# Centring a weight matrix on TensorE: full rows by zero padding, the gain in the conversion, another order of the first loads

## The chip, the cores and the metric

The kernel runs on one core of a Trainium2 chip. The metric is the device time of one launch in microseconds, the median of several runs. Below, PE is TensorE, ACT is ScalarE, DVE is VectorE, POOL is GpSimd and SP is SyncE; PEld is the weight load of a matmul.

## The reference, cut to what matters

The input x has 8 batches of 4224 rows of 192 numbers. First comes a causal convolution over rows: 7 taps, one set for each of 8 heads of 24 columns, made from `weight` by a softmax. Then a block with a layer norm, two matmuls and a residual:

```python
w = softmax(weight)                       # 8 heads x 7 taps
x = conv(x_padded_with_6_zero_rows, w)    # 8 x 4224 x 192
mu = mean(x); var = mean((x - mu)**2)
xn = (x - mu) / sqrt(var + 1e-6) * g_ln
out = x + max(xn @ w_ch1, 0) @ w_ch2      # 192 -> 768 -> 192
```

`w_ch1` and `w_ch2` come as 64-bit floats and are brought to 32 bits on the chip.

## The kernel before, in words

**Tiling.** A batch is laid out with 33 successive rows of x to each of the 128 partitions. Work goes in groups of up to 11 of these rows per partition; the first batch is cut into groups of 7, 8, 9 and 9, every other into three of 11, which makes 25 groups. For a group g the steps are: load x with 6 rows of halo (`load_x`, L91 to L107), convolve on DVE (`conv`, L245, y), transpose in blocks of 32 on DVE (`transpose`, L266, yt), multiply by w1 on PE (`up`, L315, matmul L325, four matmuls on 32 rows each beside one another, PSUM tiles ph), ReLU out of PSUM on ACT (L330, ht), multiply by w2 on PE (`down`, L335, matmul L348, PSUM tiles po), and add `rstd` times that to y on DVE (L353). `stats` (L274) computes rstd on DVE. The ReLU commutes with the positive factor rstd, so the norm's division comes last.

**Set-up.** The mean's subtraction and the gain g are folded into w1: w1 = (I - 1/192) diag(g) w_ch1, computed once by PE in `centre_w1` (L222). w_ch1 has 192 rows: the upper 128 lie in slots 1 and 2 of w1f (left and right half of the columns), the lower 64 in slot 0, the left half of the columns in partitions 0 to 63, the right half in 64 to 127. The stationary operands are the matrices centre (L209 to L220): POOL writes -1/192 and the diagonal, and ACT multiplies them by g (L219). For each of 6 blocks f of 128 columns and each of 6 blocks c of outputs, one matmul takes 128 rows (L230) and one takes the 64 rows of slot 0 that belong to f (L233); ACT copies the sums out of PSUM (L237). The trace shows each 32-bit matmul of the program as two instructions on PE: 72 here are 144.

**Conversion.** `split_words` (L152) takes the high words apart, with three operations on DVE and two on ACT (high and scale); `join_words` (L171) puts them together in three operations on DVE, the last a multiplication (L180). It is done for slots 0 and 1 (names 1a), then slot 2 (1b), later for w2 (mant, power, high, scale without a number).

**Order.** Each engine works in the order of the program text. At the end of the function: `conv(0)`, `centre_w1()`, `transpose(0)`, the conversion of w2, then per group `load_x(g+2)`, (`conv(1)` ahead of `up(0)`), `up(g)`, `conv(g+1)`, `transpose(g+1)`, `stats(g)`, `down(g)`. For groups 0 and 1 the first tap of the convolution is on ACT (L254), otherwise on DVE (L256). PSUM tiles ps are 8 buffers in a ring, for pw, ph and po alike. Loads of w1 are issued by ACT, those of the taps, x and w2 by SP, those of g by POOL.

Of the kernel before, what the change touches and what calls it, by code (L numbers as in the profile page):

```python
# [7 lines left out]
F32 = mybir.dt.float32  # L8
# [3 lines left out]
ALU = mybir.AluOpType  # L12
# [4 lines left out]
def kernel(  # L17
# [35 lines left out]
    NF = F // P  # L53
    NC = D // C
    NQ = P // C
    FH = F // 2
# [4 lines left out]
    groups = []  # L61
# [14 lines left out]
    xr = x.rearrange("b (p r) d -> b p (r d)", p=P)  # L76
# [5 lines left out]
    ypool = ctx.enter_context(tc.tile_pool(name="y", bufs=3))  # L82
# [6 lines left out]
    xg = {}  # L89

    def load_x(g):  # L91
        b, j0, n = groups[g]
        t = xpool.tile([P, J + PAD, D], F32, tag="xg", name=f"xg{g}")
        xg[g] = t
        flat = t.rearrange("p j d -> p (j d)")
        if j0:
            nc.sync.dma_start(
                out=flat[:, 0 : (n + PAD) * D], in_=xr[b, :, (j0 - PAD) * D : (j0 + n) * D]
            )
            return  # L100
        nc.gpsimd.memset(t[0:1, 0:PAD, :], 0.0)  # L101
        nc.sync.dma_start(out=flat[:, PAD * D : (PAD + n) * D], in_=xr[b, :, 0 : n * D])
        for p0, p1 in ((16, P), (1, 16)):
            nc.sync.dma_start(
                out=flat[p0:p1, 0 : PAD * D],
                in_=xr[b, p0 - 1 : p1 - 1, (R - PAD) * D : R * D],
            )  # L107

    taps = consts.tile([P, H, K], F32, name="taps")
    ga = consts.tile([P, 1], F32, name="ga")
    gb = consts.tile([P, 1], F32, name="gb")
    raw1 = setup.tile([P, 3, FH, 2], U32, name="raw1")
# [5 lines left out]
    def load_w1(r):  # L121
        nc.scalar.dma_start(  # L122
            out=raw1[:, 1 + r, :, :].rearrange("p f w -> p (f w)"),
            in_=w1_words[0:P, 2 * FH * r : 2 * FH * (r + 1)],
        )

    nc.sync.dma_start(
        out=taps, in_=bass.AP(tensor=weight.tensor, offset=0, ap=[[0, P], [K, H], [1, K]])
    )
    load_w1(0)  # L130
    for r in range(2):
        nc.scalar.dma_start(  # L132
            out=raw1[Q * r : Q * r + Q, 0, :, :].rearrange("p f w -> p (f w)"),
            in_=w1_words[P:D, 2 * FH * r : 2 * FH * (r + 1)],
        )
    load_w1(1)
    load_x(0)
    nc.gpsimd.dma_start(out=ga, in_=g_col[0:P, :])
    for r in range(2):
        nc.gpsimd.dma_start(out=gb[Q * r : Q * r + Q, :], in_=g_col[P:D, :])  # L140
# [11 lines left out]
    def split_words(raw, name):  # L152
        n = raw.shape[1]
        hi = raw[:, :, 1]
        mant = setup.tile([P, n], I32, name="mant" + name)
        power = setup.tile([P, n], I32, name="power" + name)
        high = setup.tile([P, n], F32, name="high" + name)
        scale = setup.tile([P, n], I32, name="scale" + name)
        nc.vector.tensor_single_scalar(mant.bitcast(U32), hi, 0xFFFFF, op=ALU.bitwise_and)  # L159
        nc.scalar.activation(high, mant, AF.Relu, scale=2.0**-20, bias=1.0)  # L160
# [7 lines left out]
        nc.scalar.activation(scale, power, AF.Relu, scale=float(1 << 23), bias=low)  # L168
        return high, scale

    def join_words(dst, raw, high, scale):  # L171
        lo, hi = raw[:, :, 0], raw[:, :, 1]
        nc.vector.scalar_tensor_tensor(  # L173
            out=high, in0=lo, scalar=2.0**-52, in1=high, op0=ALU.mult, op1=ALU.add
        )
# [4 lines left out]
        nc.vector.tensor_tensor(dst, high, scale.bitcast(F32), op=ALU.mult)  # L180
# [12 lines left out]
    parts_a = split_words(raw1a, "1a")  # L193
# [3 lines left out]
    nc.vector.tensor_tensor(  # L197
        taps, taps, wsum.unsqueeze(2).to_broadcast([P, H, K]), op=ALU.mult
    )
    join_words(w1f[:, 0:2].rearrange("p s f -> p (s f)"), raw1a, *parts_a)  # L200
    parts_b = split_words(raw1b, "1b")
    join_words(w1f[:, 2], raw1b, *parts_b)

# [6 lines left out]
    for i, (gk, spans) in enumerate(((ga, ((0, P, 0),)), (gb, ((0, Q, P), (Q, P, P))))):  # L210
        m = setup.tile([P, NC, NQ, C], F32, name=f"centre{i}")
        nc.gpsimd.memset(m, -1.0 / D)
        for p0, p1, base in spans:
            nc.gpsimd.affine_select(
                out=m[p0:p1], in_=m[p0:p1], pattern=[[-C, NC], [0, NQ], [-1, C]],
                compare_op=ALU.not_equal, fill=1.0 - 1.0 / D, base=base, channel_multiplier=1,
            )
        flat = m.rearrange("p c q i -> p (c q i)")
        nc.scalar.mul(flat, flat, gk)  # L219
        centre.append(flat.rearrange("p (c o) -> p c o", c=NC))  # L220

    def centre_w1():  # L222
        for f in range(NF):
            r, o = divmod(f * P, FH)
            rows = slice(Q * r, Q * r + Q)
            for c0, c1 in ((0, 4), (4, NC)):
                pw = psum.tile([P, 512], F32, tag="ps", name=f"pw{f}_{c0}")
                for c in range(c0, c1):
                    dst = pw[:, (c - c0) * P : (c - c0 + 1) * P]
                    nc.tensor.matmul(  # L230
                        dst, centre[0][:, c, :], w1f[:, 1 + r, o : o + P], start=True, stop=False
                    )
                    nc.tensor.matmul(  # L233
                        dst, centre[1][rows, c, :], w1f[rows, 0, o : o + P],
                        start=False, stop=True,
                    )
                nc.scalar.copy(  # L237
                    w1[:, c0:c1, f * P : f * P + P],
                    pw[:, 0 : (c1 - c0) * P].rearrange("p (c f) -> p c f", f=P),
                )  # L240


    y, yt, rstd = {}, {}, {}

    def conv(g):  # L245
        n = groups[g][2]
        t = xg.pop(g)
        y[g] = ypool.tile([P, J, D], F32, tag="y", name=f"y{g}")
        for k in range(K):
            for h in range(H):  # L250
                cs = slice(h * GRP, h * GRP + GRP)
                tap = taps[:, h, k : k + 1]
                if k == 0 and g < 2:
                    nc.scalar.mul(y[g][:, 0:n, cs], t[:, 0:n, cs], tap)  # L254
                elif k == 0:
                    nc.vector.tensor_scalar(  # L256
                        out=y[g][:, 0:n, cs], in0=t[:, 0:n, cs], scalar1=tap, scalar2=None,
                        op0=ALU.mult,
                    )
                else:  # L260
                    nc.vector.scalar_tensor_tensor(  # L261
                        out=y[g][:, 0:n, cs], in0=t[:, k : k + n, cs], scalar=tap,
                        in1=y[g][:, 0:n, cs], op0=ALU.mult, op1=ALU.add,
                    )

    def transpose(g):  # L266
        n = groups[g][2]
        yt[g] = tpool.tile([P, J, NC, C], F32, tag="yt", name=f"yt{g}")
        nc.vector.transpose(  # L269
            yt[g][:, 0:n].rearrange("p j c t -> p (j c t)"),  # L270
            y[g][:, 0:n].rearrange("p j d -> p (j d)"),
        )
# [90 lines left out]
                done = end  # L363


    conv(0)
    centre_w1()
    transpose(0)
    parts = split_words(raw2, "2")
    join_words(w2flat, raw2, *parts)  # L370
    for g in range(NG):
        if g + 2 < NG:
            load_x(g + 2)
        if g == 0:
            conv(1)
        up(g)
        if g + 1 < NG:
            if g > 0:
                conv(g + 1)
            transpose(g + 1)  # L380
        stats(g)
        down(g)
# [30 lines left out]
```

## Time and profile before

| what | value |
|---|---|
| time, median of 3 runs | 1118.62 us (1118.46 to 1118.95) |
| the profiled execution, its own time | 1119.14 us |
| its span, first to last instruction | 1117.3 us |
| PE busy | 1092.0 us, 98% of the span |
| DVE busy | 822.5 us, 74% |
| ACT busy | 242.0 us, 22% |
| first matmul starts | 22.01 us into the span |

The profile is one execution. A row "22.01 0.80 PE pw L230 x2" of the chain of waits reads: from 22.01 us, for 0.80 us, PE wrote pw by line 230, two instructions. A row of the groups reads: line, engine, operation, output<-inputs, shapes, count, then busy us and mean ns of one, then the idle time of the engine just before them and who ended it. A row of the stretches reads: from:to, length, and per engine busy us and (x) the number of instructions, then the granted PE clock, the share of DMA engines at work and GB/s.

### The profile page before, as it was taken

The page shows a single profiled execution, that of the slowest core. Times are in us where ns is not written, and L with a number is a line of the kernel's source. Part 1 is how long each engine was busy: PE and PEld are TensorE (multiplying, and loading weights), DVE is VectorE, ACT ScalarE, POOL GpSimd, SP SyncE. Part 2 cuts the span into 40 slices and gives each one's busy share as a digit, 9 for nine tenths or more (in the row PEclk, how much of TensorE's full clock was granted, in tenths as well). Part 3 has the DMA queues.
Part 4 walks back from the last instruction along what each step waited for, and adds up shares of the span by engine and source line. Part 5 has one row for each costly group of instructions (what it writes and reads, how often), then busy time and mean ns, then how long its engine had stood idle before and what let it go on. Part 6 is the DMA issues. An engine that isn't in the chain of part 4 may idle for free.

```text
span 1117.3 us, 24334 instructions
## 1 busy us (share of the span) xinstructions
PE 1092.0 (98%) x10512; PEld 917.0 (82%) x10512; DVE 822.5 (74%) x2362; ACT 242.0 (22%) x638; POOL 14.7 (1%) x20
## 2 busy tenths in 40 slices
PE   2999999999999999999999999999999999999998
PEld 1679998897897887887987978978978879879878
DVE  4429888869669678688697696696696786886921
ACT  3132122213113113122122032131131230221220
POOL 2000000000000000000000000000000000000000
PEclk9999999999999999999999999999999999999999
DMA  6002012202202202202102012022022022020001
GB/s 233 1 1 79 28 63 93 93 6 96 100 1 100 100 1 101 100 1 100 68 33 101 33 68 100 1 100 100 1 101 100 1 100 98 4 101 39 1 40 39
DMA packets 10475, 70.56 MB, mean 63 GB/s; under 512 B 1416, under 2 KB 2440, under 8 KB 4736
## 3 DMA queue, kind: packets, MB, share of 16 engines
q1 hardware_dynamic: 9824, 67.83, 16.6%
q8 instruction: 82, 1.34, 0.5%
q10 hardware_dynamic: 448, 1.18, 0.4%
q14 instruction: 25, 0.20, 0.1%
q0 software_dynamic: 96, 0.00, 0.0%
HBM read 43.05 MB, written 25.95 MB: 62 GB/s over the span
## 4 chain that ended last, share of the span: by engine, by line
PE 98%; DMA 1%; DVE 1%; ACTq 0%; ACT 0%; issue 0%; DVEq 0%
PE po L348 47%; PE ph L325 46%; PE pw L230 2%; PE pw L233 2%; DMA raw<-in_moe_w_ch_dram 1%; DVE w1f L180 0%; ACT centre L219 0%; DVE scale1a L176 0%; DVE high1a L173 0%; DVE power1a L165 0%; DVE mant1a L159 0%; ACTq L132 0%; DVE power1a L161 0%; DVE y L353 0%; ACTq L122 0%
## 5 line engine op out<-in xcount | busy, mean ns | idle before, releaser
L348 PEld LDWEIGHTS po<-w,ht 128*128 128x128 f32 x3168 | 513.5, 190 | 13.3 <-issue 11.7
L348 PE MATMUL po<-w,ht 128*128 128x192 f32 x3168 | 522.5, 327 | 0.0
L325 PE MATMUL ph<-yt,w 32*128 32x352 f32 (+3 forms) x7200 | 520.8, 445 | 0.0
L325 PEld LDWEIGHTS ph<-yt,w 32*128 32x128 f32 x7200 | 367.6, 186 | 145.4 <-issue 5.6
L261 DVE SCALAR_TENSOR_TENSOR y<-xg,taps,y 128x264 f32<-128x264 f32 (+3 forms) x1200 | 473.8, 477 | 0.9 <-ACT y L254 0.9
L330 ACT ACTIVATE ht<-ph 128x352 f32<-128x352 f32 (+3 forms) x600 | 222.7, 457 | 791.6 <-PE ph L325 791.6
L353 DVE SCALAR_TENSOR_TENSOR y<-po,r,y 128x192 f32<-128x192 f32 x264 | 96.6, 413 | 230.0 <-PE po L348 226.9
L282 DVE BATCH_NORM_STATS2 st<-y 128x6 f32<-128x192 f32 x264 | 70.1, 340 | 0.0
L269 DVE STREAM_TRANSPOSE yt<-y 128x2112 f32<-128x2112 f32 (+3 forms) x25 | 57.3, 2290 | 0.9
L256 DVE TENSOR_SCALAR y<-xg,taps 128x264 f32<-128x264 f32 (+1 forms) x184 | 51.4, 351 | 0.0
L230 PE MATMUL pw<-w1f,centre 128*128 128x128 f32 x72 | 28.6, 501 | 22.0 <-ACT centre L219 22.0
L230 PEld LDWEIGHTS pw<-w1f,centre 128*128 128x128 f32 x72 | 18.0, 310 | 29.9 <-ACT centre L219 22.0
L233 PE MATMUL pw<-w1f,centre 64*128 64x128 f32 x72 | 28.5, 498 | 0.0
L173 DVE SCALAR_TENSOR_TENSOR high<-raw,high 128x1152 f32<-128x1152 uint32 x1 | 1.4, 1358 | 34.1 <-ACT high L160 34.1
L233 PEld LDWEIGHTS pw<-w1f,centre 64*128 64x128 f32 x72 | 18.0, 310 | 8.2 <-issue 7.9
L101 POOL MEMSET xg<- 1x1152 f32 x8 | 8.4, 1047 | 819.6 <-DVE y L261 819.3
L237 ACT COPY w<-pw 128x512 f32<-128x512 f32 (+1 forms) x12 | 5.8, 479 | 43.5 <-PE pw L233 43.5
L304 DVE TENSOR_TENSOR d<-r 128x11 f32<-128x11 f32 (+3 forms) x75 | 12.8, 170 | 2.6
L305 DVE SCALAR_TENSOR_TENSOR d<-d,v 128x11 f32<-128x11 f32 (+3 forms) x75 | 12.8, 170 | 2.6
L308 DVE SCALAR_TENSOR_TENSOR r<-d,r 128x11 f32<-128x11 f32 (+3 forms) x75 | 12.7, 170 | 2.6
L159 DVE TENSOR_SCALAR mant1a<-raw 128x768 uint32<-128x768 uint32 x1 | 0.6, 560 | 7.3 <-DMA raw<-in_moe_w_ch_dram 7.3
L254 ACT ACTIVATE y<-xg,taps 128x168 f32<-128x168 f32 (+1 forms) x16 | 5.6, 433 | 0.0
(48 smaller groups left out, 58.7 us busy)
## 6 DMA issues: line engine op xcount, KB each, us to landing
xg<-in_x_dram SPq DMA_DIRECT2D x14, 1632.0 KB, 9.3
out_dram<-y SPq DMA_DIRECT2D x20, 1056.0 KB, 4.9
xg<-in_x_dram SPq DMA_DIRECT2D x7, 1056.0 KB, 7.9
xg<-in_x_dram SPq DMA_DIRECT2D x8, 504.0 KB, 9.2
xg<-in_x_dram SPq DMA_DIRECT2D x2, 1440.0 KB, 11.2
out_dram<-y SPq DMA_DIRECT2D x2, 864.0 KB, 4.4
xg<-in_x_dram SPq DMA_DIRECT2D x1, 1344.0 KB, 12.7
raw<-in_moe_w_ch_dram SPq DMA_DIRECT2D x1, 1152.0 KB, 10.0
```

What stands on the lines that cost most here:

```text
L230: nc.tensor.matmul(dst, centre[0][:, c, :], w1f[:, 1 + r, o : o + P], start=True, stop=False)
L233: nc.tensor.matmul(dst, centre[1][rows, c, :], w1f[rows, 0, o : o + P], start=False, stop=True,)
L256: nc.vector.tensor_scalar(out=y[g][:, 0:n, cs], in0=t[:, 0:n, cs], scalar1=tap, scalar2=None, op0=ALU.mult,)
L261: nc.vector.scalar_tensor_tensor(out=y[g][:, 0:n, cs], in0=t[:, k : k + n, cs], scalar=tap, in1=y[g][:, 0:n, cs], op0=ALU.mult, op1=ALU.add,)
L269: nc.vector.transpose(yt[g][:, 0:n].rearrange("p j c t -> p (j c t)"), y[g][:, 0:n].rearrange("p j d -> p (j d)"),)
L282: nc.vector.bn_stats(out=st[:, j, :], in_=y[g][:, j, :])
L304: nc.vector.tensor_tensor(d, r, r, op=ALU.mult)
L305: nc.vector.scalar_tensor_tensor(out=d, in0=d, scalar=-0.5, in1=v, op0=ALU.mult, op1=ALU.mult)
L325: nc.tensor.matmul(ph[q][:, 0 : n * C], w1[rows, c, fs], t[rows, 0:n, c, :], start=(c == 0), stop=(c == NC - 1),)
L330: nc.scalar.activation(ht[g][:, f, 0:n, q, :], ph[q][:, 0 : n * C].rearrange("p (j t) -> p j t", t=C), AF.Relu,)
L348: nc.tensor.matmul(dst, t[:, f, j, :, :].rearrange("p q t -> p (q t)"), w2[:, f, :], start=(f == 0), stop=(f == NF - 1),)
L353: nc.vector.scalar_tensor_tensor(out=yg[:, j, :], in0=dst, scalar=rstd[g][:, j : j + 1], in1=yg[:, j, :], op0=ALU.mult, op1=ALU.add,)
```

## The change

The lower 64 rows no longer get matmuls of 64 rows. There are three centre matrices: the first for the upper 128 rows, the second for the lower rows with the left half (partitions 64 to 127 are zero), the third for the lower rows with the right half (partitions 0 to 63 are zero). Each matmul of `centre_w1` then reads 128 rows, and the zeros cancel what does not belong to f. The gain g no longer goes into the centre matrices on ACT, but into w1f on DVE: the last multiplication of `join_words` becomes `scalar_tensor_tensor` (high times g times scale), in two pieces of 384 columns for 1a, one for 1b. The loads of g are issued first on POOL. w1 comes by one transfer of the upper 128 rows and one of 64 rows from ACT, and one of 64 rows from SP, which stands ahead of x there. The halo of x at the start of a batch comes with the rows themselves, in one piece per partition (two transfers by partitions, and one for partition 0). The first tap is a function of its own; its call for group 1 stands ahead of the conversion of w2.

```diff
-        nc.sync.dma_start(out=flat[:, PAD * D : (PAD + n) * D], in_=xr[b, :, 0 : n * D])
         for p0, p1 in ((16, P), (1, 16)):
             nc.sync.dma_start(
-                out=flat[p0:p1, 0 : PAD * D],
-                in_=xr[b, p0 - 1 : p1 - 1, (R - PAD) * D : R * D],
+                out=flat[p0:p1, 0 : (PAD + n) * D],
+                in_=bass.AP(
+                    tensor=x.tensor, offset=(b * S + p0 * R - PAD) * D,
+                    ap=[[R * D, p1 - p0], [1, (PAD + n) * D]],
+                ),
             )
+        nc.sync.dma_start(out=flat[0:1, PAD * D : (PAD + n) * D], in_=xr[b, 0:1, 0 : n * D])
...
-    load_w1(0)
+    nc.scalar.dma_start(
+        out=raw1[:, 1:3].rearrange("p s f w -> p (s f w)"), in_=w1_words[0:P, :]
+    )
     for r in range(2):
-        nc.scalar.dma_start(
+        (nc.sync, nc.scalar)[r].dma_start(
             out=raw1[Q * r : Q * r + Q, 0, :, :].rearrange("p f w -> p (f w)"),
             in_=w1_words[P:D, 2 * FH * r : 2 * FH * (r + 1)],
         )
-    load_w1(1)
     load_x(0)
...
-        nc.vector.tensor_tensor(dst, high, scale.bitcast(F32), op=ALU.mult)
+        if gain is None:
+            nc.vector.tensor_tensor(dst, high, scale.bitcast(F32), op=ALU.mult)
+            return
+        n = dst.shape[1] // len(gain)
+        for i, g in enumerate(gain):
+            part = slice(n * i, n * i + n)
+            nc.vector.scalar_tensor_tensor(
+                out=dst[:, part], in0=high[:, part], scalar=g, in1=scale.bitcast(F32)[:, part],
+                op0=ALU.mult, op1=ALU.mult,
+            )
...
-    join_words(w1f[:, 0:2].rearrange("p s f -> p (s f)"), raw1a, *parts_a)
+    join_words(w1f[:, 0:2].rearrange("p s f -> p (s f)"), raw1a, *parts_a, (gb, ga))
     parts_b = split_words(raw1b, "1b")
-    join_words(w1f[:, 2], raw1b, *parts_b)
+    join_words(w1f[:, 2], raw1b, *parts_b, (ga,))
...
+    for i, (p0, p1, base) in enumerate(((0, P, 0), (0, Q, P), (Q, P, P))):
         m = setup.tile([P, NC, NQ, C], F32, name=f"centre{i}")
...
-        nc.scalar.mul(flat, flat, gk)
-        centre.append(flat.rearrange("p (c o) -> p c o", c=NC))
+        if p1 - p0 < P:
+            nc.gpsimd.memset(m[P - p1 : P - p0], 0.0)
+        nc.gpsimd.memset(m[p0:p1], -1.0 / D)
...
-                    nc.tensor.matmul(
-                        dst, centre[0][:, c, :], w1f[:, 1 + r, o : o + P], start=True, stop=False
-                    )
-                    nc.tensor.matmul(
-                        dst, centre[1][rows, c, :], w1f[rows, 0, o : o + P],
-                        start=False, stop=True,
-                    )
+                    for m, s, start in ((centre[0], 1 + r, True), (centre[1 + r], 0, False)):
+                        nc.tensor.matmul(
+                            dst, m[:, c, :], w1f[:, s, o : o + P], start=start, stop=not start
+                        )
...
+    first_tap(0)
     conv(0)
     centre_w1()
+    first_tap(1)
     transpose(0)
```

What moves on the engines is seen in their rows. ACT at the start of the program, before: after its loads of w1 (raw) it converts (1a, 1b), multiplies two centre matrices by g, takes the first tap of group 0 and begins to copy the centred w1 (w) out of PSUM.

```order
L122 DMA raw_84<-in_moe_w_ch_dram 128x768
L132 DMA raw_84<-in_moe_w_ch_dram 64x768 x2
L122 DMA raw_84<-in_moe_w_ch_dram 128x768
...
L168 ACTIVATE scale1b<-power1b,low 128x384
L219 ACTIVATE centre_140<-centre_140,ga 128x768
L219 ACTIVATE centre_146<-centre_146,gb 128x768
L254 ACTIVATE y_155<-xg_91,taps 128x7x24 x8
L237 COPY w_138<-pw_0_212 128x4x128
```

The same place with the change:

```order
L130 DMA raw_84<-in_moe_w_ch_dram 128x1536
L134 DMA raw_84<-in_moe_w_ch_dram 64x768
...
L166 ACTIVATE scale1b<-power1b,low 128x384
L255 ACTIVATE y_157<-xg_93,taps 128x7x24 x8
L240 COPY w_138<-pw_0_214 128x4x128
```

Four transfers have become two, and the two multiplications of centre are gone. ACT after the last copy of the centring, before: the two operations for w2 (high, scale), the first tap of group 1, the first ReLU.

```order
L237 COPY w_138<-pw_4_302 128x2x128
L160 ACTIVATE high_312<-mant_310 128x1152
L168 ACTIVATE scale_313<-power_311,low 128x1152
L254 ACTIVATE y_324<-xg_100,taps 128x8x24 x8
L330 ACTIVATE ht_381<-ph_0_0_382 128x7x32
```

And with the change:

```order
L240 COPY w_138<-pw_4_304 128x2x128
L255 ACTIVATE y_310<-xg_99,taps 128x8x24 x8
L158 ACTIVATE high_323<-mant_321 128x1152
L166 ACTIVATE scale_324<-power_322,low 128x1152
L334 ACTIVATE ht_383<-ph_0_0_384 128x7x32
```

The eight multiplications of the first tap of group 1 now stand ahead of the two for w2. On SP's queue the loads at the start, before: taps, x of group 0 in three transfers (xg_91), w2 (raw_85), x of group 1.

```order
L127 DMA taps<-in_weight_dram 128x56
L102 DMA xg_91<-in_x_dram 128x1344
L104 DMA xg_91<-in_x_dram 112x1152
L104 DMA xg_91<-in_x_dram 15x1152
L141 DMA raw_85<-in_moe_w_ch_dram 128x6x384
L97 DMA xg_100<-in_x_dram 128x2688
```

And with the change:

```order
L127 DMA taps<-in_weight_dram 128x56
L134 DMA raw_84<-in_moe_w_ch_dram 64x768
L103 DMA xg_93<-in_x_dram 112x2496
L103 DMA xg_93<-in_x_dram 15x2496
L110 DMA xg_93<-in_x_dram 1x1344
L139 DMA raw_85<-in_moe_w_ch_dram 128x6x384
L97 DMA xg_99<-in_x_dram 128x2688
```

A part of w1 (raw_84) stands ahead of x, and x of group 0 comes with its halo.

More of the change, by code (lines that the diff above doesn't have):

```diff
@@ L119 @@
     g_col = moe_g_ln.rearrange("(d o) -> d o", o=1)
-    def load_w1(r):
-        nc.scalar.dma_start(
-            out=raw1[:, 1 + r, :, :].rearrange("p f w -> p (f w)"),
-            in_=w1_words[0:P, 2 * FH * r : 2 * FH * (r + 1)],
-        )
+    nc.gpsimd.dma_start(out=ga, in_=g_col[0:P, :])
+    for r in range(2):
+        nc.gpsimd.dma_start(out=gb[Q * r : Q * r + Q, :], in_=g_col[P:D, :])
     nc.sync.dma_start(
@@ L129 @@
     )
-    load_w1(0)
+    nc.scalar.dma_start(
+        out=raw1[:, 1:3].rearrange("p s f w -> p (s f w)"), in_=w1_words[0:P, :]
+    )
     for r in range(2):
-        nc.scalar.dma_start(
+        (nc.sync, nc.scalar)[r].dma_start(
             out=raw1[Q * r : Q * r + Q, 0, :, :].rearrange("p f w -> p (f w)"),
@@ L135 @@
         )
-    load_w1(1)
     load_x(0)
-    nc.gpsimd.dma_start(out=ga, in_=g_col[0:P, :])
-    for r in range(2):
-        nc.gpsimd.dma_start(out=gb[Q * r : Q * r + Q, :], in_=g_col[P:D, :])
     nc.sync.dma_start(
@@ L169, in split_words, with join_words @@
         return high, scale
-    def join_words(dst, raw, high, scale):
+    def join_words(dst, raw, high, scale, gain=None):
         lo, hi = raw[:, :, 0], raw[:, :, 1]
@@ L209 @@
     centre = []
-    for i, (gk, spans) in enumerate(((ga, ((0, P, 0),)), (gb, ((0, Q, P), (Q, P, P))))):
+    for i, (p0, p1, base) in enumerate(((0, P, 0), (0, Q, P), (Q, P, P))):
         m = setup.tile([P, NC, NQ, C], F32, name=f"centre{i}")
[L212 to L216, printed above, removed]
-            )
-        flat = m.rearrange("p c q i -> p (c q i)")
-        nc.scalar.mul(flat, flat, gk)
-        centre.append(flat.rearrange("p (c o) -> p c o", c=NC))
+        if p1 - p0 < P:
+            nc.gpsimd.memset(m[P - p1 : P - p0], 0.0)
+        nc.gpsimd.memset(m[p0:p1], -1.0 / D)
+        nc.gpsimd.affine_select(
+            out=m[p0:p1], in_=m[p0:p1], pattern=[[-C, NC], [0, NQ], [-1, C]],
+            compare_op=ALU.not_equal, fill=1.0 - 1.0 / D, base=base, channel_multiplier=1,
+        )
+        centre.append(m.rearrange("p c q i -> p c (q i)"))
     def centre_w1():
@@ L224, in centre_w1 @@
             r, o = divmod(f * P, FH)
-            rows = slice(Q * r, Q * r + Q)
             for c0, c1 in ((0, 4), (4, NC)):
@@ L229, in centre_w1 @@
                     dst = pw[:, (c - c0) * P : (c - c0 + 1) * P]
-                    nc.tensor.matmul(
-                        dst, centre[0][:, c, :], w1f[:, 1 + r, o : o + P], start=True, stop=False
-                    )
-                    nc.tensor.matmul(
-                        dst, centre[1][rows, c, :], w1f[rows, 0, o : o + P],
-                        start=False, stop=True,
-                    )
+                    for m, s, start in ((centre[0], 1 + r, True), (centre[1 + r], 0, False)):
+                        nc.tensor.matmul(
+                            dst, m[:, c, :], w1f[:, s, o : o + P], start=start, stop=not start
+                        )
                 nc.scalar.copy(
@@ L243, with first_tap @@
     y, yt, rstd = {}, {}, {}
+    def first_tap(g):
+        n = groups[g][2]
+        y[g] = ypool.tile([P, J, D], F32, tag="y", name=f"y{g}")
+        for h in range(H):
+            cs = slice(h * GRP, h * GRP + GRP)
+            dst, src, tap = y[g][:, 0:n, cs], xg[g][:, 0:n, cs], taps[:, h, 0:1]
+            if g < 2:
+                nc.scalar.mul(dst, src, tap)
+            else:
+                nc.vector.tensor_scalar(out=dst, in0=src, scalar1=tap, scalar2=None, op0=ALU.mult)
     def conv(g):
@@ L247, in conv @@
         t = xg.pop(g)
-        y[g] = ypool.tile([P, J, D], F32, tag="y", name=f"y{g}")
-        for k in range(K):
+        for k in range(1, K):
             for h in range(H):
                 cs = slice(h * GRP, h * GRP + GRP)
[L252 to L264, printed above, removed]
+                nc.vector.scalar_tensor_tensor(
+                    out=y[g][:, 0:n, cs], in0=t[:, k : k + n, cs], scalar=taps[:, h, k : k + 1],
+                    in1=y[g][:, 0:n, cs], op0=ALU.mult, op1=ALU.add,
+                )
     def transpose(g):
@@ L378 @@
             if g > 0:
+                first_tap(g + 1)
                 conv(g + 1)
```

## Prediction

> **What bounds the kernel now.** The page comes first: PE is busy almost from its first instruction to the last, and the chain that ended last is PE.
>
> ```profile
> span 1117.3 us, 24334 instructions
> PE 98%; DMA 1%; DVE 1%; ACTq 0%; ACT 0%; issue 0%; DVEq 0%
> ```
>
> So a microsecond counts only if it is taken from PE's line: from the start until PE runs, from what PE does, or from a wait put into it. The chain of waits in order of time shows that line at the start, where the whole change lies.
>
> ```profile
> 1.76 12.48 DMA raw<-in_moe_w_ch_dram
> ...
> 18.59 0.96 DVE w1f L180
> ...
> 21.04 0.93 ACT centre L219
> ...
> 22.01 0.80 PE pw L230 x2
> ...
> 73.54 0.72 PE pw L233 x2
> 74.27 16.20 PE ph L325 x288
> 90.47 13.85 PE po L348 x84
> 104.32 15.75 PE ph L325 x288
> ```
>
> Until 14.24 us w1 arrives, until 19.55 DVE converts it, until 21.97 PE waits for ACT's centre. Centring takes 74.27 - 22.01 = 52.26 us for 144 instructions, 0.363 us each. Then come up(0), down(0) and, at 104.32, up(1). Is 0.363 us what such a matmul must take? The groups of the page answer it.
>
> ```profile
> L348 PEld LDWEIGHTS po<-w,ht 128*128 128x128 f32 x3168 | 513.5, 190 | 13.3 <-issue 11.7
> L348 PE MATMUL po<-w,ht 128*128 128x192 f32 x3168 | 522.5, 327 | 0.0
> L230 PE MATMUL pw<-w1f,centre 128*128 128x128 f32 x72 | 28.6, 501 | 22.0 <-ACT centre L219 22.0
> L233 PE MATMUL pw<-w1f,centre 64*128 64x128 f32 x72 | 28.5, 498 | 0.0
> ```
>
> L348 loads weights of the same 128x128 and streams 192 columns, in 522.5 / 3168 = 0.165 us each; pw streams 128 and takes 2.2 times as long. Two reasons can be read. First, PE's timeline by single instructions, and that of the weight loads:
>
> ```profile
> 26.46 0.58 PE L230 MATMUL pw<-w1f,centre 128*128 128x128 f32 x1
> 26.46 0.79 PE L230 MATMUL pw<-w1f,centre 128*128 128x128 f32 x2
> 25.73 0.50 PEld L233 LDWEIGHTS pw<-w1f,centre 64*128 64x128 f32 x2 [0.23 <-issue]
> ```
>
> Within a pair of one line the second matmul ends 27.25 - 27.04 = 0.21 us after the first. Between pairs, where 128 rows give way to 64 or back, weight loading stands idle for 0.23 us with nothing shown to wait for: there PE empties itself first. Second, up(0) by stretches of time, one line and one shape throughout:
>
> ```profile
> 74.20:76.60 2.40, 2.40 (x25) 2.27 (x29) 1.00 0.01 3
> 76.60:79.00 2.40, 2.40 (x32) 2.27 (x28) 1.00 0.00 0
> 79.00:81.40 2.40, 2.40 (x56) 2.40 (x52) 1.00 0.03 7
> ```
>
> At 79.0 us PE doubles its pace (32 to 56 in 2.4 us), though the clock column says 1.00 throughout; so up to there PE ran at half speed, through all of the centring. The Trainium skill, "TensorE: Matmul & The Clock Gate", Part 1, says that PE starts at half clock and is released after some 3.4 us of sustained work; here 52 us of broken work released nothing, and 4.8 us of dense work did.
>
> **The change part by part.**
>
> *The padded matmuls.* All 144 now use 128 rows, so the 0.23 us between pairs goes. At half speed one costs the 0.21 us inside a pair, at full speed 0.165 x 128 / 192 = 0.110 us, if the weight load hides as it does in L348. Upper bound for full speed: the whole 0.165, as L348 does the same load and more columns in that. I take 4.8 us at half speed (as up(0) needed), which is 4.8 / 0.21 = 23 instructions, and 121 x 0.110 = 13.3 us: 18.1 us against 52.26. Zeros cost nothing by the row count: 64 and 128 rows take 498 and 501 ns. And PE is already at speed in up(0): 57 instructions took 4.8 us there, later 2.4, so up(0) takes 16.2 - 2.4 = 13.8 us.
>
> *The start.* Two stretches of time (the last number is GB/s) and the issues of w1:
>
> ```profile
> 4.00:7.00 3.00, 0.00 (x0) 0.00 (x0) 0.50 (x2) 1.28 (x1) 2.85 (x4) 1.00 0.88 313
> 7.00:10.00 3.00, 0.00 (x0) 0.00 (x0) 0.12 (x1) 0.25 (x1) 1.07 (x2) 1.00 1.04 231
> raw<-in_moe_w_ch_dram ACTq DMA_DIRECT2D x2, 384.0 KB, 9.9
> raw<-in_moe_w_ch_dram ACTq DMA_DIRECT2D x2, 192.0 KB, 11.9
> ```
>
> DVE's timeline up to the first additions out of PSUM:
>
> ```profile
> 14.38 0.56 DVE L159 TENSOR_SCALAR mant1a<-raw 128x768 uint32<-128x768 uint32 x1 [7.25 <-DMA raw<-in_moe_w_ch_dram]
> 21.76 0.56 DVE L180 TENSOR_TENSOR w1f<-high1b,scale1b 128x384 f32<-128x384 f32 x1
> 23.22 14.76 DVE L261 SCALAR_TENSOR_TENSOR y<-xg,taps,y 128x168 f32<-128x168 f32 x48 [0.90 <-ACT y L254]
> 38.01 1.58 DVE L269 STREAM_TRANSPOSE yt<-y 128x1344 f32<-128x1344 f32 x1
> 39.52 0.72 DVE L159 TENSOR_SCALAR mant<-raw 128x1152 uint32<-128x1152 uint32 x1
> 75.77 1.36 DVE L173 SCALAR_TENSOR_TENSOR high<-raw,high 128x1152 f32<-128x1152 uint32 x1 [34.07 <-ACT high L160]
> 79.71 15.88 DVE L261 SCALAR_TENSOR_TENSOR y<-xg,taps,y 128x192 f32<-128x192 f32 x48
> 95.63 1.78 DVE L269 STREAM_TRANSPOSE yt<-y 128x1536 f32<-128x1536 f32 x1
> 97.33 1.88 DVE L282 BATCH_NORM_STATS2 st<-y 128x6 f32<-128x192 f32 x7
> 102.34 2.43 DVE L353 SCALAR_TENSOR_TENSOR y<-po,r,y 128x192 f32<-128x192 f32 x7
> ```
>
> w1 is 2 x 384 + 2 x 192 = 1152 KB, 1.18 MB; x of group 0 with halo is 13 x 192 x 4 bytes x 128, 1.28 MB. Had w1 the 313 GB/s from 4 us to itself, it would be there at 7.8; if all of x came with it at the mean of both stretches (272), at 13.0. I take the middle, 10.4, and mant1a at 10.6 instead of 14.38. Bounds: 8.4 (the loads of g, though first, need their time too) and 14.38 (no gain; all of w1 is now awaited at once, also what came later as 1b). Two pieces with gain in place of L180 (0.96): at most 2 x 0.56, +0.15 us. With ACT's multiplications gone, PE starts at w1f: 10.6 + (19.55 - 14.38) + 0.15 = 15.9 us, and centring ends at 34.1. POOL has the g loads ahead and three more operations (two memsets, one matrix); it was at work for only 1.07 us of 7 to 10, so some 3 us more end before 15.9.
>
> *What is late next.* DVE: conv(0) starts behind 1b, at 10.6 + (22.32 - 14.38) + 0.15 = 18.7, takes 14.8 and ends at 33.5; its transpose ends at 35.1. So up(0) starts at 35.1: the convolution, which had 35 us to spare, is last now, 1.0 us behind PE. Every microsecond of w1's landing counts one to one; PE's own cold time does not, up to 1.0 us.
>
> *The moved first tap of group 1.* Nothing that waits is in front of it but PE's last copy.
>
> ```profile
> 20.52 0.62 ACT L168 ACTIVATE scale1b<-power1b,low 128x384 int32<-128x384 int32 x1
> 74.30 0.37 ACT L237 COPY w<-pw 128x256 f32<-128x256 f32 x1 [2.31 <-PE pw L233]
> 74.57 1.17 ACT L160 ACTIVATE high<-mant 128x1152 f32<-128x1152 int32 x1
> 75.64 1.25 ACT L168 ACTIVATE scale<-power,low 128x1152 int32<-128x1152 int32 x1
> 76.78 2.86 ACT L254 ACTIVATE y<-xg,taps 128x192 f32<-128x192 f32 x8
> 79.55 1.06 ACT L330 ACTIVATE ht<-ph 128x224 f32<-128x224 f32 x4
> ```
>
> ACT ends copying at 34.5, the tap at 37.4, then high and scale (2.3) at 39.7; behind these queues the first ReLU, until 40.8. up(0) has written all 8 PSUM buffers after two of six blocks, at 35.1 + 2 x 2.3 = 39.7, and waits there for 1.1 us. It ends at 35.1 + 13.8 + 1.1 = 50.0. DVE takes w2 up 1.2 us after ACT began (as 74.57 to 75.77): 38.6, w2 done at 42.5 (3.94 later, as 75.77 to 79.71), in time for down(0) at 50.0, which ends at 63.85. Then conv(1) until 58.5, its transpose until 60.2 (in time for up(1)), stats until 65.2, and the additions out of PSUM until 67.5. up(1) starts at 63.85, and its second block, 15.75 / 6 = 2.6 us later at 66.5, needs the four buffers of po: a wait of 1.0 us. Before, those were free at 104.77, for 106.95. So up(1) is as if started at 64.85, against 104.32: 39.5 us earlier. Over the whole span DVE is busy for 822.5 us where PE is for 1092 (the table above), so it falls no further behind; PE runs the same instructions.
>
> *x in one row.* In the later batches the bytes are the same and the loads two groups ahead; nothing that PE waits for.
>
> **The sum.** -39.5 us on 1119.14 is 1079.6 us; the profiled execution is 0.5 us over the median of the runs, which the range covers.
>
> **The rivals.**
>
> *A: the weight load does not hide.* The Trainium skill, same page, Part 3, says that a weight load overlaps running matmuls only where the row groups differ; all matmuls of the centring would now use all rows. By rows, exposed or not, load and 128 columns fit into 0.165 us at full speed, 0.33 at half: 15 + 129 instructions, 26.1 us, end at 42.0, and with the same steps for ACT and DVE (ReLU wait 2.1, PSUM wait 1.0) up(1) as if at 72.9: 1087.7 us. By the page's figure, 128 / 1.2 = 107 ns on top of each, it would be an estimated 0.217 each. Against it: L348 has all rows, and its loads are busy for 513.5 us beside matmuls busy for 522.5.
>
> *B: the clock is not released in the centring.* 144 x 0.214 = 30.8 us, end at 46.7, up(0) at 16.2 as before: up(1) as if at 77.4, 1092.2 us. Against it: up(0) was released by dense work.
>
> *C: the change doesn't do what it says*, as the 0.23 us belong to a new weight or sum, not to the rows. Then centring stays at 52.26 and the gain is the start: 6.1 us less a PSUM wait of 0.8, 1113.8 us. Against it: new sums in L348 leave no gap.
>
> *D, slower: a matmul costs by its rows*, and 64 padded to 128 doubles 72 of them: 72 x 0.363 = +26.1, less 5.3 of the start: 1140 us. It decides from 5.3 / 72 = 0.074 us more per padded matmul. The 498 against 501 ns speak against it.
>
> **How the numbers follow.** The forecast has a chance of 0.80, A 0.06, B 0.06, C 0.05, D 0.02, anything else 0.01. Its own range: landing at 8.4 or 14.38 gives -2.2 or +3.8; the two waits can vanish (-2.1) or double (+2.1); so 1075.3 to 1085.5. To 1089 it takes A in: 1075 to 1089. No change that can be told is within 0.2%, about what a measurement of this kernel resolves. Faster: all but D and the rest, 0.97; same 0.01; slower 0.02.
>
> **What would show it.** Right: pw at about 0.11 us after a few us at twice that, no idle time of weight loading between pairs, up(0) at 56 in 2.4 us from its first stretch and started by DVE's transpose, up(1) near 65 us. Wrong: pw at 0.2 to the end (B), gaps after every second matmul (C), mant1a no earlier than 14, or PE waits in groups 2 and 3 for yt.

## The result, and the profile after

The changed kernel takes 1081.32 us (median of 4 runs, 1080.26 to 1082.69), the kernel before 1118.78 us beside it (1118.46 to 1119.1): a ratio of 0.9666, 95% interval 0.9649 to 0.9683, 37.5 us less. The profiled execution took 1082.24 us, 36.9 less than that of before; the sum had said 39.5 and 1079.6. First the page: PE is still the kernel, and its span is 36.8 us shorter.

```profile
span 1080.5 us, 24335 instructions
PE 96%; DVE 2%; DMA 1%; issue 0%; ACT 0%; ACTq 0%; DVEq 0%
```

The chain of waits in order of time shows what is new: DVE, not PE, now leads from w1 to up(0).

```profile
1.20 11.83 DMA raw<-in_moe_w_ch_dram
...
13.16 0.56 DVE mant1a L157
...
17.37 1.15 DVE w1f L184 x2
...
21.27 14.70 DVE y L265 x48
...
35.99 1.59 DVE yt L273
...
37.71 14.71 PE ph L329 x283
52.43 13.85 PE po L352 x84
66.27 16.88 PE ph L329 x288
```

No pw is in it: the centring ends ahead of the transpose. up(1) starts at 66.27 and takes 16.88 instead of 15.75 us, and the 1.13 us more are read as its forecast wait; so it is as if started at 67.4, against 104.32 before: 36.9 us, the whole gain. The groups of the page (L237 are the padded matmuls, L329 is up):

```profile
L329 PE MATMUL ph<-yt,w 32*128 32x352 f32 (+3 forms) x7200 | 520.4, 444 | 1.0 <-DVE yt L273 1.0
L237 PE MATMUL pw<-w1f,centre 128*128 128x128 f32 x144 | 18.0, 292 | 18.7 <-DVE w1f L184 18.7
L237 PEld LDWEIGHTS pw<-w1f,centre 128*128 128x128 f32 x144 | 17.9, 208 | 18.6 <-issue 18.6
```

The 144 matmuls are busy for 18.0 us, where the forecast said 18.1, and the loads of their weights for 17.9 beside them. Where the speed changes is seen in L237 by stretches of 2 us:

```profile
18.70:20.70 2.00, 2.00 (x9) 2.00 (x10) 1.00 1.07 442
20.70:22.70 2.00, 2.00 (x14) 2.00 (x13) 1.00 1.02 432
22.70:24.70 2.00, 2.00 (x21) 2.00 (x20) 1.00 0.96 409
34.70:36.70 2.00, 1.99 (x18) 1.80 (x17) 1.00 0.00 0
```

9 in 2 us at first (0.21 us from start to start), 18 at the end (0.11); the change lies at 22.25 us, 3.6 us after the first matmul at 18.66. And up(0) has its full pace from its first stretch (51 in 2.4 us, against 25 before):

```profile
37.70:40.10 2.40, 2.39 (x51) 2.40 (x54) 1.00 0.00 0
```

ACT's timeline behind the last copy shows the forecast wait for a ReLU: it starts at 41.97, when up(0) has written its first two blocks.

```profile
36.73 0.37 ACT L240 COPY w<-pw 128x256 f32<-128x256 f32 x1 [0.31 <-PE pw L237]
36.99 2.88 ACT L255 ACTIVATE y<-xg,taps 128x192 f32<-128x192 f32 x8
39.77 1.15 ACT L158 ACTIVATE high<-mant 128x1152 f32<-128x1152 int32 x1
40.83 1.25 ACT L166 ACTIVATE scale<-power,low 128x1152 int32<-128x1152 int32 x1
41.97 2.04 ACT L334 ACTIVATE ht<-ph 128x224 f32<-128x224 f32 x8
```

### The profile page after: what moved, and what is told of

It reads as the page before. It is cut to its first block, busy times and chain, and to the rows that moved or that the text cites. A ratio compares the mean times of both kernels' runs of the same rounds, so it can differ in the third digit from the quotient of the medians.

```text
span 1080.5 us, 24335 instructions
## 1 busy us (share of the span) xinstructions
PE 1057.4 (98%) x10512; PEld 898.8 (83%) x10512; DVE 822.2 (76%) x2363; ACT 240.3 (22%) x636; POOL 16.9 (2%) x23
## 4 chain that ended last, share of the span: by engine, by line
PE 96%; DVE 2%; DMA 1%; issue 0%; ACT 0%; ACTq 0%; DVEq 0%
PE po L352 48%; PE ph L329 48%; DVE y L265 1%; DMA raw<-in_moe_w_ch_dram 1%; DVE yt L273 0%; DVE w1f L184 0%; DVE scale1a L174 0%; ACT scale1b L166 0%; DVE scale1b L174 0%; DVE power1a L163 0%; DVE mant1a L157 0%; DVE power1a L159 0%; DVE y L357 0%; ACTq L130 0%; DVE power1b L163 0%
## 5 line engine op out<-in xcount | busy, mean ns | idle before, releaser
L329 PE MATMUL ph<-yt,w 32*128 32x352 f32 (+3 forms) x7200 | 520.4, 444 | 1.0 <-DVE yt L273 1.0
L329 PEld LDWEIGHTS ph<-yt,w 32*128 32x128 f32 x7200 | 367.4, 185 | 146.1 <-issue 5.4
L237 PE MATMUL pw<-w1f,centre 128*128 128x128 f32 x144 | 18.0, 292 | 18.7 <-DVE w1f L184 18.7
L237 PEld LDWEIGHTS pw<-w1f,centre 128*128 128x128 f32 x144 | 17.9, 208 | 18.6 <-issue 18.6
L289 DVE TENSOR_TENSOR d<-st 128x11 f32<-128x11 f32 (+3 forms) x25 | 4.4, 177 | 0.9
L300 DVE TENSOR_SCALAR d<-v 128x11 uint32<-128x11 uint32 (+3 forms) x25 | 4.3, 173 | 0.9
L297 DVE TENSOR_SCALAR v<-v 128x11 f32<-128x11 f32 (+3 forms) x25 | 4.3, 173 | 0.9
```

What stands on the lines that cost most here:

```text
L237: nc.tensor.matmul(dst, m[:, c, :], w1f[:, s, o : o + P], start=start, stop=not start)
L329: nc.tensor.matmul(ph[q][:, 0 : n * C], w1[rows, c, fs], t[rows, 0:n, c, :], start=(c == 0), stop=(c == NC - 1),)
```

## The experiments

The theory is the prediction's: alternating 128 and 64 rows empties PE at each change and keeps its clock at half, and behind the padding DVE's chain from w1's landing sets the time. Runs of the changed kernel spread over 2.4 us, so differences below 2 us are read at their places in the traces; "up(1) as if started" is its start plus what it takes over 15.75 us.

### Padding alone

```diff
-    for i, (gk, spans) in enumerate(((ga, ((0, P, 0),)), (gb, ((0, Q, P), (Q, P, P))))):
+    for i, (gk, p0, p1, base) in enumerate(((ga, 0, P, 0), (gb, 0, Q, P), (gb, Q, P, P))):
...
-                        dst, centre[1][rows, c, :], w1f[rows, 0, o : o + P],
+                        dst, centre[1 + r][:, c, :], w1f[:, 0, o : o + P],
```

> The kernel before with the zero padding alone (three centre matrices, all still multiplied by g on ACT; loads, conversion and order of before). Theory, that the alternation of 128 and 64 rows empties PE and keeps its clock at half: the 144 matmuls still start near 22.0 us but take about 18.6 us as in the changed kernel, not 52.3; conv(0) starts 0.8 us later behind a third multiplication on ACT, its transpose ends near 40.4, up(0) starts there, the first ReLU holds it up by some 2.6 us, up(1) starts near 71: about 1085.5 us (1083 to 1089). Rival, that the gain comes from the loads, the gain in the conversion and the order: the matmuls stay at 0.36 us each and the time within 1117 to 1121.

Measured: 1084.53 us (1084.2 to 1084.86) against 1117.92, ratio 0.970 (0.9685 to 0.9714). Its groups:

```profile
L231 PE MATMUL pw<-w1f,centre 128*128 128x128 f32 x72 | 15.0, 292 | 21.3 <-ACT centre L220 21.3
L234 PE MATMUL pw<-w1f,centre 128*128 128x128 f32 x72 | 14.8, 289 | 0.0
```

And its chain from up(0) on:

```profile
46.12 10.06 PE ph L326 x187
56.19 13.85 PE po L349 x84
70.03 15.75 PE ph L326 x288
```

Both lines now take 290 ns where they took 500, and up(1) starts at 70.03 (expected 71). The padding alone is worth 33.4 of the 37 us.

### Everything but the padding

```diff
-                    for m, s, start in ((centre[0], 1 + r, True), (centre[1 + r], 0, False)):
...
+                        dst, centre[1 + r][rows, c, :], w1f[rows, 0, o : o + P],
+                        start=False, stop=True,
```

> The changed kernel without the padding alone: the lower rows by matmuls of 64 rows again, alternating with those of 128. Theory: 0.363 us for each of the 144, 52 us from 18.6 to 70.9, weight loading idle for 0.22 us between pairs, half speed until some 5 us into up(0); up(0) then starts 3.4 us earlier than before, of which the moved first tap gives back some 0.8: 1116 us (1114.5 to 1118). Rival, the loads and the order are what counts: below 1090.

Measured: 1114.79 us (1114.12 to 1116.84), ratio 0.9972 (0.9962 to 0.9982): 3.1 us faster than before. The timeline of its weight loads shows the gaps again:

```profile
29.98 0.50 PEld L240 LDWEIGHTS pw<-w1f,centre 64*128 64x128 f32 x2 [0.23 <-issue]
30.70 0.50 PEld L237 LDWEIGHTS pw<-w1f,centre 128*128 128x128 f32 x2 [0.22 <-issue]
```

up(0) starts at 71.28. So the loads, the gain in the conversion and the order are worth 3 us by themselves; the rival that gave them the gain has fallen.

### Without padding, rows grouped

```diff
                 for c in range(c0, c1):
...
+                        dst, centre[0][:, c, :], w1f[:, 1 + r, o : o + P],
+                        start=c == c0, stop=False,
+                    )
+                for c in range(c0, c1):
...
+                        dst, centre[1 + r][rows, c, :], w1f[rows, 0, o : o + P],
+                        start=False, stop=c == c1 - 1,
```

> The changed kernel without padding, but within each PSUM tile first the 4 (or 2) matmuls of 128 rows, then those of 64: 23 changes of the row count instead of 71, all else as without padding (the sums of a tile are opened by its first matmul alone). Theory, that the change of the row count costs: 18.6 us plus 23 x 0.15 to 0.3 us, so 22 to 25.5 us of centring, the clock released within it, and 1085 to 1089 us. Rival one, that a matmul of 64 rows or each new weight costs the gap: 52 us as with alternation, about 1116. Rival two, that the gap goes but the clock stays at half: 31 + 7 = 38 us, about 1103.

Measured: 1100.37 us (1099.91 to 1102.32), ratio 0.9845 (0.983 to 0.9859). PE's timeline in the centring:

```profile
31.47 2.07 PE L237 MATMUL pw<-w1f,centre 128*128 128x128 f32 x8
33.47 2.07 PE L243 MATMUL pw<-w1f,centre 64*128 64x128 f32 x8
```

And up(0) in its chain:

```profile
56.77 16.24 PE ph L336 x288
```

Eight matmuls start 2.00 us apart from the next eight: 8 x 0.2135 and 0.295 us for the change of rows, alike for 64 and 128 rows. In all 144 x 0.2135 + 24 x 0.295 = 37.8 us, and 56.77 - 18.88 = 37.89 are seen. So the gap belongs to the change of the row count, not to a new weight, a new sum or to 64 rows. But the first theory missed: the clock stayed at half, as rival two said (about 1103 us expected), though the gaps were down to 0.3 us in 2.

### What releases the clock: dummies of 128 and of 64 rows

Two versions of the changed kernel put matmuls of zeros ahead of the centring, where PE was idle; nothing reads their sums.

```diff
+    idle = setup.tile([P, P], F32, name="idle")
+    nc.vector.memset(idle, 0.0)
...
+    pi = psum.tile([P, 512], F32, tag="ps", name="pi")
+    for _ in range(60):
+        nc.tensor.matmul(pi[:, 0:P], idle, idle, start=True, stop=True)
     first_tap(0)
```

The second has `range(40)` and `idle[0:Q]` for both operands.

> The changed kernel with 60 matmuls of zeros (128 rows, 128 columns, into a PSUM tile that nothing reads) ahead of the centring, so that PE is at full speed when it starts. Theory: the dummies run for 4 to 5 us at 0.21 and then at 0.11 us each and are done by 17; the centring takes 16.1 instead of 18.6 us, but up(0) waits for the transpose all the same, now for 3 us, and the time is that of the changed kernel, 1080 to 1082.7. Rival, that the cold stretch of PE counts: 2.5 us faster, below 1079.5. If the longer wait puts the clock back, up(0) starts at half speed and it is up to 2.4 us slower.

> As the run with dummies of 128 rows, but with 40 dummies of 64 rows each, without any gap between them. It tells why the clock stayed at half when the rows were grouped. Theory, that the rows at work count for the release: the dummies stay at 0.21 us, 17 us in all, and the centring starts at half speed. Rival, that only the gaps count: the dummies reach 0.11 us after 4 to 5 us, as those of 128 rows do.

PE's timeline with dummies of 128 rows, 1079.98 us (1079.6 to 1080.95; ratio to before 0.9662, 0.9648 to 0.9675):

```profile
1.10 15.70 PE L374 MATMUL pi<-idle 128*128 128x128 f32 x120 [1.10 <-DVE idle L150]
18.59 16.32 PE L239 MATMUL pw<-w1f,centre 128*128 128x128 f32 x144 [1.79 <-DVE w1f L186]
37.63 13.90 PE L331 MATMUL ph<-yt,w 32*128 32x224 f32 x288 [2.73 <-DVE yt L275]
```

And with those of 64 rows (one run, 1082.04 us):

```profile
1.10 17.43 PE L374 MATMUL pi<-idle 64*128 64x128 f32 x80 [1.10 <-DVE idle L150]
18.46 17.92 PE L239 MATMUL pw<-w1f,centre 128*128 128x128 f32 x144
```

80 dummies of 64 rows take 0.218 us each for 17 us without a gap and the clock is not released; it is 3.3 us into the 128-row matmuls that follow. The dummies of 128 rows hold zeros too and were released after 4.3 us, so it is not the values. So the number of rows counts, not only the gaps. That this is why grouping did not do what padding did is argued and not shown apart: no run had rows of 128 throughout with the gaps of the grouped run. The Trainium skill, "TensorE: Matmul & The Clock Gate", Part 1, asks for some 3.4 us of sustained activity: for 128 rows the traces agree roughly (the release came 2.9 to 5.5 us after the first such matmul, over all runs), for 64 rows 17 us were not enough.

The warm start also tested "PE's own cold time does not count": up(0) waits 2.73 us for the transpose and starts at 37.63 as expected, but up(1) is as if started at 66.1 (65.38 + 16.48 - 15.75), 1.3 us earlier than with the change at nearly the same landing (13.08 against 13.16). The cold time counts by another way: the copies end earlier, so does the tap, and conv(1) starts at 43.58 instead of 44.89. The medians, 1079.98 and 1081.32, do not tell it from nothing.

### Alternation with a warm clock

The kernel without padding, with the 60 dummies of 128 rows ahead.

> The kernel without padding, alternating 128 and 64 rows, with 60 matmuls of zeros of 128 rows ahead, so that PE is at full speed when the centring starts. It tells how much of the 52 us the clock is. Theory, that the alternation cannot hold the clock: some 3 to 7 us at full speed, then 0.363 each again, so 45 to 50 us in all. Rival, that it holds once released: each pair of pairs then costs its matmuls at 0.11 us and a gap, some 0.18 to 0.26 each, 26 to 37 us in all.

One run, 1113.65 us. The centring starts at 18.14 and up(0) at 68.10, so it took 50.0 us, as the theory said:

```profile
68.10 15.90 PE ph L335 x288
```

PE's timeline at full speed:

```profile
18.94 0.49 PE L239 MATMUL pw<-w1f,centre 128*128 128x128 f32 x2
19.36 0.48 PE L242 MATMUL pw<-w1f,centre 64*128 64x128 f32 x2
```

PE by stretches of 3 us, where the clock column does say it:

```profile
18.10:21.10 3.00, 2.96 (x15) 1.00 1.07 442
21.10:24.10 3.00, 3.00 (x9) 0.50 1.01 428
```

Six pairs take 2.50 us at full speed (18.53 to 21.03), 0.417 us each: 2 x 0.112 and 0.193 for the change. The clock is lost after 3 us. With that the 52.3 us of before come apart: 144 x 0.112 = 16.1 us of matmuls, 72 x 0.193 = 13.9 us of changes, and the rest, 22.3 us, the half clock. This split prices the changes at full clock. Priced at half clock they are 72 x 0.295 = 21.2 us, and the half clock of the matmuls themselves is 144 x (0.2135 - 0.112) = 14.6 us. So which part is the larger depends on the order, and as the alternation itself kept the clock down, no run here had the one without the other.

### The first tap put back

```diff
-    first_tap(1)
     transpose(0)
     parts = split_words(raw2, "2")
+    first_tap(1)
     join_words(w2flat, raw2, *parts)
```

> The changed kernel with the first tap of group 1 behind the conversion of w2 on ACT again, as before. Theory by the same sum as the forecast: up(0) starts at 37.7 as with the change, its wait for PSUM grows from 1.0 to about 2.5 us as the first ReLU stands behind high, scale and the tap, but w2 is ready 1.3 us earlier on DVE and the wait of 1.1 us in up(1) goes: +0.4 us in all, within 0.2%. Rival, that the moved tap is worth 2 us or more, as it frees conv(1): 1083.5 or more against 1081.3.

Measured: 1081.01 us (1080.92 to 1083.06), ratio 0.9668 (0.9652 to 0.9684). PE's waits:

```profile
PE ph L329 <- ACT ht L334: 1.5, 1, 1.5
```

And up(1) in its chain:

```profile
68.21 15.75 PE ph L329 x288
```

up(0) waits longer, up(1) no longer (15.75 us), as the sum said. From mant1a (13.43) it is 54.8 us to up(1), with the change 54.2: the moved tap is worth 0.5 us, below what the times tell.

### x in three transfers again

The changed kernel with the lines of `load_x` from before (128 partitions of rows, then the halo).

> The changed kernel with x loaded as before at the start of a batch (128 partitions of rows, then the halo by itself); everything else as changed. Theory, that the rows with halo in 112 and 15 partitions are what made x slow and held up w1 (9984 bytes took 740 ns each there, while 10752 bytes of the next load, in 128 partitions, took 404): mant1a starts at 11.5 to 12.5 instead of 13.2 to 13.4, and the time is 1079.5 to 1080.5 (the changed kernel: 1081.3). Rival, that w1 waits for the same bytes either way: mant1a between 13.0 and 13.8, 1081 to 1082.

Measured: 1081.02 us (1080.9 to 1081.57), ratio 0.9671 (0.9657 to 0.9684). DVE's timeline where w1 has landed:

```profile
11.40 0.56 DVE L154 TENSOR_SCALAR mant1a<-raw 128x768 uint32<-128x768 uint32 x1 [4.47 <-DMA raw<-in_moe_w_ch_dram]
```

And its chain:

```profile
16.91 18.48 PE pw L234 x144
35.41 0.37 ACT w L237
35.78 2.77 ACT y L252 x8
...
64.96 16.90 PE ph L326 x288
```

w1 lands 1.8 us earlier than with the change; the eight traces with the loads of the change have mant1a at 12.63 to 13.65, so the new form of x is what holds it up. The stretch from 7 to 10 us had 179 GB/s with the change and has 232 here. But the time hardly moves: up(1) is as if started at 66.1, 1.3 us earlier. The chain now goes by PE's centring and ACT's copies and tap, so with an earlier landing these are late next.

### w1 ahead of x in one queue

```diff
+        queue = nc.scalar if g < 2 else nc.sync
...
-            nc.sync.dma_start(
+            queue.dma_start(
```

The issue of w2 moves to ACT in the same way.

> The changed kernel with x of groups 0 and 1 and w2 issued by ACT, in one queue behind w1, so that no x moves beside w1. Theory, that x beside it is what holds w1 up, and that every microsecond of its landing counts one to one: mant1a at 7.5 to 9 us; the loads of g, which landed near 12.5 before, then set the last step of the conversion, so the matmuls start near 14 and up(0) near 33 instead of 37.7: 1076 to 1078 us. Rival, that w1 is slow by itself (its own rows, or the small packets of taps and g): mant1a after 12, and 1081 to 1083.

Measured: 1081.83 us (1079.8 to 1082.1), ratio 0.9672 (0.9659 to 0.9685). DVE's timeline:

```profile
11.61 0.56 DVE L158 TENSOR_SCALAR mant1a<-raw 128x768 uint32<-128x768 uint32 x1 [4.70 <-DMA raw<-in_moe_w_ch_dram]
...
21.23 14.84 DVE L266 SCALAR_TENSOR_TENSOR y<-xg,taps,y 128x168 f32<-128x168 f32 x48 [1.43 <-ACT y L256]
```

And L330 (up) by stretches of 2.4 us:

```profile
37.80:40.20 2.40, 2.37 (x32) 2.40 (x36) 0.63 0.00 0
40.20:42.60 2.40, 2.40 (x40) 2.40 (x36) 0.66 0.01 3
42.60:45.00 2.40, 2.40 (x59) 2.40 (x56) 1.00 0.04 7
```

The theory missed: w1 does not land at 7.5 to 9 but at 11.6, no earlier than with x in three transfers beside it. But the edit does not do what it was meant to do: x still moves beside w1. In the packets of this trace the first one of x (9984 bytes) starts at 7.19 us and the last one of w1 (3072 bytes) ends at 10.25; from 7 to 10 us 37 packets of x are at work. So one queue did not keep them apart, and what w1 takes by itself was not measured. The small packets of g and the pieces of 64 rows were at work then too, and what each of the three costs is left open. And x now comes late: conv(0) waits 1.43 us and the convolution starts at 21.23 as with the change. Meanwhile PE stands idle for 2.4 us between centring and up(0) (35.45 to 37.83), and the clock falls back to half from 38.41 to 41.82: 32 instructions in 2.4 us.

### One cut of x moved

```diff
-        for p0, p1 in ((16, P), (1, 16)):
+        for p0, p1 in ((8, P), (1, 8)):
```

> The changed kernel with one number changed: the rows of x at the start of a batch are cut at partition 8 instead of 16, so 120 and 7 (and 1) partitions instead of 112 and 15 (and 1). Theory, that x is slow where the cut gives the DMA engines 7 partitions each instead of 8: its 9984 bytes take near 400 ns instead of 740, those of later batches (13056 bytes) near 500 instead of 710 to 770, the other transfers beside it go faster too, and mant1a starts near 11.5 instead of 13.1 to 13.4, all of x being there by 13; the time is near that of the run with x in three transfers, 1081 (1080 to 1081.5). Rival, that any x in less than 128 partitions, or the bytes, are what counts: 650 ns or more, mant1a after 12.8.

Measured: 1080.91 us (1080.2 to 1084.04), ratio 0.9675 (0.9662 to 0.9689). In its profile, which is of the slowest of the four executions, mant1a starts at 14.24, packets of 9984 bytes take 778 ns each and those of 13056 bytes in later batches some 900 (with the change 740 and 700 to 770, for 128 partitions some 500). The time is as expected, but the theory of 7 against 8 partitions has fallen, and the rival holds. That x in 127 partitions is slower than in 128 is seen in every batch; why, stays open.

### A version meant to beat both

The cut at 8, 50 dummies, and the tap between the copies:

```diff
                     pw[:, 0 : (c1 - c0) * P].rearrange("p (c f) -> p c f", f=P),
                 )
+            if f == 3:
+                first_tap(1)
```

> A version meant to beat the changed kernel: the cut at partition 8, 50 matmuls of zeros ahead of the centring, and the first tap of group 1 on ACT between the copies of the fourth and the fifth block of the centring. Theory, that behind the centring ACT is what DVE and PE wait for: the tap is hidden in ACT's idle time, high and scale follow the last copy at once, up(0) does not wait for a ReLU and conv(1) starts near 42 instead of 44.9; up(1) starts near 64 with a wait below 0.6: 1077.5 to 1079. If x lands no earlier, the gain is 1.5 us less. Rival, that the copies delayed by the tap hold PE up, or that nothing is won as DVE's chain is as long: 1080.5 or more.

> The changed kernel itself once more, on the same chip and in the same rounds as the two runs ahead: 1080 to 1083, mant1a between 12.8 and 13.7.

Measured: 1080.39 us (1079.37 to 1080.55), ratio to before 0.9661 (0.9648 to 0.9674); the changed kernel beside it 1082.08 (1080.22 to 1082.32), 0.9677 (0.9664 to 0.969). The chain of the new version:

```profile
37.24 13.90 PE ph L333 x288
51.15 13.85 PE po L356 x84
65.00 16.47 PE ph L333 x288
```

up(0) no longer waits for a ReLU (13.90 us), and up(1) is as if started at 65.7 against 67.5 beside it (66.34 + 16.88 - 15.75): 1.7 us, which is also the difference of the medians. 0.8 of it is the landing (mant1a at 12.69 against 13.51 beside it), so the tap and the dummies have 0.9. The intervals overlap, so it is not clear in the times. The expected 1077.5 to 1079 was missed; for x landing no earlier, 1.5 us more had been said, which fits. mant1a lies within the 12.63 to 13.65 of the other traces, so the cut at 8 is not seen to help. The clock was also lost again while PE waited 4.1 us for w1 behind the dummies, so the centring took 17.9 us:

```profile
L239 PE MATMUL pw<-w1f,centre 128*128 128x128 f32 x144 | 17.9, 291 | 4.1 <-DVE w1f L186 4.1
```

## Why the prediction was right, point by point

**The padded matmuls.** Right in mechanism and size: 18.0 us against 18.1, 0.21 us each for 3.6 us and then 0.11, up(0) at full pace from the start. What the prediction read as two reasons are two, and the runs give their sizes: with the changes priced at full clock, the 34 us are 13.9 of changes of the row count and 22.3 of the clock, less 1.9 for the cold stretch left. That 64 rows do not release the clock even without gaps was not in the prediction.

**The start.** This is the term that was mis-sized: mant1a forecast at 10.6, seen at 13.16 (12.63 to 14.24 over the runs with x in one row beside w1). It is 2.56 us, the whole miss (39.5 forecast, 36.9 seen). The step that failed is the middle between "w1 alone" and "all of x with it" at the rate of before: from 4 to 7 and from 7 to 10 us 273 and 179 GB/s were moved, where before 313 and 231 were, and in the second stretch x in one piece, which is slower, took its share. With x behind it in its own queue, yet still beside it in time, w1 came at 11.6. The bound of 14.38 was the better guide.

**What is late next.** Right: from mant1a to up(0) the sum said 24.5 us, and 24.55 are seen (13.16 to 37.71); the wait for the transpose was forecast at 1.0 and is 1.0. But that PE's cold time is free held for up(0) alone: by ACT's copies, tap and w2 it counts 1.3 us in up(1), in the one trace of the warm start.

**The moved tap and the waits.** ReLU wait 1.1 forecast, up(0) took 14.71 instead of 13.8, 0.9; PSUM wait 1.0 forecast, 1.13 seen. From mant1a to up(1) as if started 54.25 us were forecast and 54.24 are seen; the steps are right to 0.2 us each, and that their small errors cancel is luck.

**The rivals.** A fell: at 0.112 us for a load and 128 columns of all rows, the load hides, and the rule of the Trainium skill that it does so only for other row groups ("TensorE: Matmul & The Clock Gate", Part 3) does not hold here. B fell for the padded matmuls, though it is just what happened when the rows were grouped. C fell by the run without padding and by the grouped rows, D by 0.2135 us for either row count.

## What to carry to other kernels

Where short matmuls alternate between 128 and 64 rows, look at the weight loads for idle time put down to "issue" and at the pace of one line over time: zeros that keep all rows cost nothing in time here and can win back the clock as well as the gaps. A stage that shrinks by 34 us hands the end to whatever was hidden in it, so the gain ahead of it is to be read from that chain, from its first transfer on. And of a load that is only moved forward among the same bytes, take little until a trace shows it.

## What the runs showed of the hardware

- A change between 128 and 64 rows costs 0.295 us at half clock and 0.19 us at full, in either direction. The Trainium skill, "TensorEngine Tiling (Array Packing)", Tiling Modes, says that a change of tiling mode drains TensorE; the traces agree and give the price.
- 64-row matmuls without a gap did not release the clock in 17 us; 128-row ones did in 2.9 to 5.5 us. Once released, alternation lost it after 3 us, and an idle stretch of 2.4 us lost it in one run, one of 2.73 us in another did not.
- The spread has a pattern in the traces. The stretches between two changes of the granted clock last 3.41, 13.65, 17.07, 51.20 or 1037 us and more, in every trace a whole multiple of 3.413 us. Cut into such steps from a change, the release came behind a step with 2.91 us or more of dense work (rows of 128, or up's four times 32), and not behind one with 2.09; the loss came behind steps with 1.03 us of work or none, or with alternation, and not behind one with 1.63. The idle 2.4 us of the run with w1 first lie in one step (35.00 to 38.41), the 2.73 us of the warm start across two (cut at 36.12).
- The record of the clock begins with its first release (79.06 us in before, 22.25 with the change), and the column reads 1.00 ahead of that, as in the whole centring of before; there only the pace of instructions shows half speed.
- x in 112 and 15 partitions moved slower than in 128: with the change 740 ns for 9984 bytes at the start (beside other loads), and 700 to 770 for 13056 bytes in later batches, where 128 partitions took some 500.
